# Half as many opening products on TensorE, each twice as wide

## The chip, the cores and the metric

The kernel runs on one core of a Trainium2 chip, in one launch. The time is the device time of that core in microseconds (us), the median of several runs. The profile is of one separate execution, and times inside it are counted from its first instruction.

## The reference

One transformer block on 2048 rows of width 512, in bfloat16: a pre-norm linear attention with 32 heads of 16, and a pre-norm dense block of width 1792 with a ReLU.

```python
def _A_ref(x, wqkv, wo):                       # linear attention
    qkv = (x @ wqkv).reshape(B, S, 3, H, Dh).transpose(2, 0, 3, 1, 4)
    q, k, v = qkv[0], qkv[1], qkv[2]
    phi = lambda t: jnp.where(t > 0, t + 1, jnp.exp(t)) + 1e-6
    pq, pk = phi(q), phi(k)
    kv = jnp.einsum("bhsd,bhse->bhde", pk, v)
    z = jnp.einsum("bhsd->bhd", pk)
    num = jnp.einsum("bhqd,bhde->bhqe", pq, kv)
    den = jnp.einsum("bhqd,bhd->bhq", pq, z)[..., None] + 1e-6
    return (num / den).transpose(0, 2, 1, 3).reshape(B, S, D) @ wo
...
h = x + _A_ref(_layernorm(x), A_wqkv, A_wo)
h2 = h + relu(_layernorm(h) @ B_w1) @ B_w2     # the result
```

## The kernel before

The 2048 rows are 16 tiles of 128, in four chunks of 512 rows. The program is a list of short words, `ORDER`, that is written out by hand. Each word is one step, a call of the function `op_` plus the word's name with the word's numbers, and the steps are recorded in the list's order; each engine runs its own instructions in that order, and waits on semaphores for what it needs. So the list fixes the order on every engine, SyncE's DMA issues among them, and nothing is rearranged later.

The steps at the start, which are those that the change and the prediction touch:

- `warm.n.b.w` (L243 to L245) runs n products on TensorE (PE) of a 128x128 block of zeros with w columns of zeros, into PSUM bank b. Nobody reads what they leave there; `start=True` makes the next user of the bank overwrite it. `warm.2.7` leaves w at 512. The zeros are the tile `zeros`, which is the first quarter of `m_sb`; `op_const` (L185) sets its first 128 columns with one VectorE memset (L186) and the other 384 with a later one (L190). Each product is a pair of instructions, a weight load (PEld) and a matmul.
- `lx` loads rows of x (L214), `lk` and `lq` the weights of k and q (`wk_sb`, `wq_sb`, L220), all by SyncE (SP), in the order of the list: x three times, wk, x three times, wq, and so on.
- `S`, `A`, `R`, `N` normalise a tile: statistics on VectorE (DVE; L248, L249), the inverse root on ScalarE (ACT; L254, L255), and the normalised tile into `h_nat` on VectorE (L262).
- `T` transposes a tile with four products of 128 columns (L287), `E` copies the transposed tile to `lnT` on ScalarE (L297).
- `K` is a tile's product with the k weights, four products of 512 columns (L316), `Q` a block of q for a whole chunk, four products of 512 (L324).

On TensorE the list begins: 70 products of 64 columns, two of 512, then T.0, T.1, K.0, T.2, K.1, T.3, K.2, and the first of the q products, Q.0.3, which is the first step that needs `wq_sb`. Behind it come more K and Q, the sum over all rows of k against the normalised tile (L368), small products for the attention's state (L392, L414, L426, L440), the attention's output (L493), and the dense block (L508 and L517 for its first product, L537 for its second). `wb` and `rb` (L468, L471) take the reciprocal of the denominators through DRAM into `rr`, and `dm` (L484) multiplies by it; each chunk's `h` products (L493) wait for that.

The only lines of the program that differ are the first warm word, and, in form alone, how `start` and `stop` of two products are computed.

Of the kernel before, what the change touches and what calls it, by code (L numbers as in the profile page):

```python
# [15 lines left out]


ORDER = """
table const masks warm.70.7.64 warm.2.7 lx.0.1 S.0 A.0 R.0.1 lx.1.1 S.1 lx.2.1 A.1 N.0 T.0.1 lk.0.4 S.2 R.1.1
N.1 T.1.2 lx.3.1 A.2 E.0 K.0.4 R.2.1 lx.4.2 S.3 N.2 T.2.1 E.1 A.3 S.5 R.3.1 K.1.0.0.2 K.1.0.2.2 N.3 S.4 A.5 A.4  # L20
E.2 T.3.2 K.2.6.0.2 K.2.6.2.2 F.0.1 M.0.1 lx.6.2 E.3 S.7 lq.0.4 R.4.2 lx.8.4 Q.0.3.1 N.4 U.0.1 A.7 F.1.1 F.2.1
T.4.2 N.5 S.6 Q.0.1.4 U.1.1 M.1.1 A.6 lx.12.4 M.2.1 D.0.1 R.6.2 K.3.7.0.2 K.3.7.2.2 E.4 X.5 U.2.1 U.3.1 D.1.1
N.6 Q.0.0.3 N.7 S.10 qF.0.0.2 K.4.5 K.5.6 S.8 A.10 S.9 A.8 qU.0.0.2 S.12 F.4.2 D.2.1 X.6 Q.0.2.0 A.9 A.12 K.6.2
S.13 S.11 M.4.2 A.11 A.13 U.4.2 D.4.2 F.3.1 R.8.2 N.9 M.3.1 X.7 K.7.3 R.12.2 R.10.2 N.8 F.6.2 D.3.1 N.13 S.15
G.0 G.1 U.6.2 S.14 X.9 X.8 N.10 A.14 A.15 N.12 qM.0.0.2 M.6.2 X.13 qF.0.2.2 R.14.2 qU.0.2.2 qM.0.2.2 N.11 G.2
G.3 G.5 G.4 N.14 X.12 K.9.3 K.8.2 K.13.1 N.15 qD.0.0.2 D.6.2 za.4.1 X.11 X.10 F.8.2 U.8.2 M.8.2 K.12.0 U.12.2
F.12.2 G.7 za.6.0 K.11.3 D.8.2 qD.0.2.2 M.12.2 za.8.0 K.10.2 F.10.2 X.14 G.8 K.14.0 U.10.2 X.15 K.15.1 M.10.2 zf
lv.2.2 lv.0.2 G.9 D.10.2 zhi D.12.2 F.14.2 G.6 G.10 G.11 M.14.2 zlo U.14.2 D.14.2 z.0.0 z.2.0 z.3.0 z.1.0 G.14
lo.0.2 lo.2.2 zc zh d4.0.1 dl4.0 l1.0.2 G.13 G.12 G.15 dx4.0 gA.2.2 Q.1.1.3 Q.1.0.2 qF.1.0.2 gD.0.2 kv.1.4
kv.3.4 kv.0.4 kv.2.4 kx qU.1.0.2 qM.1.0.2 qD.1.0.2 Q.1.3.1 Q.1.2.0 qF.1.2.2 m.0.2 m.1.3 mD.0.2 m.3.7 m.2.6 wb.0  # L30
Q.2.0.4 Q.2.1.5 rb.0.7 rb.0.1 rb.0.6 rb.0.3 rb.0.0 rb.0.2 rb.0.4 rb.0.5 l1.2.2 qM.1.2.2 qU.1.2.2 Q.2.3.1
qD.1.2.2 mA.2.2 qF.2.0.2 Q.2.2.0 qU.2.0.2 dm.0.2.2 dm.0.0.2 qM.2.0.2 h.1.6 hD.1 s.1 a.1 qU.2.2.2 d4.1.3 dl4.1
h.0.7 hD.0 s.0 dx4.1 h.2.6 h.3.5 a.0 l2.0.7 wb.1 hD.2 nA.1 hD.3 qF.2.2.2 nA.0 s.2 s.3 Q.3.0.2 Q.3.1.3 a.2
Q.3.3.6 a.3 qF.3.0.2 qU.3.0.2 Q.3.2.5 x.1 r.0.4 qF.3.2.2 n.2 t.2.7 n.3 t.3.4 qD.2.0.2 v.2 v.3 x.0 ph.0.3.1.0
ph.0.1.3.0 ph.0.2.0.0 ph.0.3.1.1 qM.2.2.2 qM.3.0.2 ph.0.0.2.0 ph.0.0.2.1 qM.3.2.2 qD.3.0.2 qU.3.2.2 qD.2.2.2
ph.0.2.0.1 qD.3.2.2 p.0.7.5 d4.2.6.2 pD.0.2.2 dl4.2 dl4.3 rb.1.4 rb.1.6 rb.1.3 rb.1.2 rb.1.0 rb.1.1 ph.0.1.3.1
rb.1.7 rb.1.5 p.0.6.4 dx4.2 dm.1.0.2 dm.1.2.2 h.4.0 pD.0.0.2 hD.4 pD.0.6.2 p.0.5.1 h.6.6 dx4.3 p.0.4.0 hD.6
l2.7.7 h.5.4 pA.0.4.2 s.4 s.6 hD.5 h.7.7 a.4 a.6 p.0.11.6 p.0.10.5 s.5 hD.7 a.5 p.0.9.4 wb.2 rb.2.6 n.4 rb.2.0
rb.2.4 s.7 n.6 rb.2.3 rb.2.2 rb.2.1 a.7 n.5 n.7 rb.2.5 rb.2.7 dm.2.0.2 dm.2.2.2 pD.0.10.2 p.0.13.1 p.0.12.0
p.0.8.3 pD.0.12.2 wb.3 r.4.4 rb.3.0 rb.3.4 h.10.7 hD.10 x.6 h.8.2 h.11.6 hD.8 s.10 rb.3.5 rb.3.1 rb.3.6  # L40
f.1.0.0.7 rb.3.3 rb.3.2 rb.3.7 s.8 hD.11 pD.0.8.2 h.9.5 f.3.1.0.7 x.7 x.5 s.11 a.8 hD.9 f.1.0.7.7 f.0.4.0.7 a.10
a.11 x.4 dm.3.2.2 dm.3.0.2 h.14.7 h.12.3 s.9 n.11 h.15.6 a.9 n.10 h.13.2 fo.1 n.9 n.8 hD.14 s.14 hD.12 x.11
hD.15 f.0.4.7.7 r.8.4 p.1.13.7 p.1.6.3 a.14 hD.13 s.12 s.15 s.13 a.12 a.15 a.13 n.14 p.1.12.6 n.13 f.3.1.7.7
n.12 n.15 p.1.2.5 fo.0 pD.1.12.2 x.10 p.1.7.4 fo.3 p.1.3.6 x.9 pD.1.6.2 pD.1.2.2 r.12.4 x.8 p.1.11.2 p.1.10.1
pD.1.10.2 f.2.4.0.7 p.2.0.6 p.2.1.7 f.2.4.7.7 pD.2.0.2 p.2.10.0 p.2.11.1 fo.2 x.14 p.2.6.2 p.2.7.3 x.15 fd.3
p.2.13.7 p.2.12.6 pD.2.10.2 pD.2.6.2 x.12 fd.1 pD.2.12.2 p.2.2.0 x.13 fd.0 p.2.3.1 p.1.5.6 p.1.4.5 pD.2.2.2
pD.1.4.2 p.1.0.3 p.1.1.4 p.1.9.1 p.1.8.0 pD.1.0.2 pD.1.8.2 f.4.4.0.7 f.4.4.7.7 fo.4 fd.4 f.5.3.0.7 f.5.3.7.7
fo.5 fd.2 f.6.7.0.7 f.6.7.7.7 fo.6 p.2.4.2 p.2.5.3 f.7.0.0.7 f.7.0.7.7 pD.2.4.2 fo.7 p.3.6.1 p.3.7.2 pD.3.6.2
p.3.8.3 p.3.9.4 p.3.5.1 pD.3.8.2 p.3.4.0 pD.3.4.2 fd.6 p.3.10.3 p.3.11.4 pD.3.10.2 p.3.2.0 p.3.3.1 p.3.0.5
p.3.1.6 pD.3.2.2 pD.3.0.2 p.3.13.3 fd.7 p.3.12.2 pD.3.12.2 f.10.1.0.7 f.15.2.0.14.3.1 f.15.7.0.14.0.2 p.2.8.4  # L50
p.2.9.5 fo.15.3.1 fd.15.3.1 fo.15.0.2 pD.2.8.2 f.8.7.0.7 f.10.1.7.7 fo.10 f.8.7.7.7 fo.8 f.14.2.0.7 f.14.2.7.7
f.13.3.0.7 fd.5 fd.8 fd.10 fo.14 f.13.3.7.7 fo.13 f.9.0.0.7 f.9.0.7.7 fd.15.0.2 f.11.6.0.7 f.11.6.7.7 fd.13 fo.9
f.12.0.0.7 fd.9 f.12.0.7.7 fo.11 fd.14 fd.11 fo.12 fd.12 f.15.2.0.14.2.1 fo.15.2.1 fd.15.2.1
"""


# [1 line left out]
def kernel(  # L58
# [14 lines left out]
    S, D = xf.shape  # L73
# [7 lines left out]
    KD = D // P  # L81
    KF = FF // P
# [5 lines left out]
    const = ctx.enter_context(tc.tile_pool(name="const", bufs=1))  # L88
# [58 lines left out]
    rb = big.tile([P, NE, 2, CW], BF16, name="rb")  # L147
# [10 lines left out]
    def pk(t, n=1):  # L158
        return pk_lo[:, t : t + n, :] if t < 2 else acts[0][:, t - 2 : t - 2 + n, :]
# [9 lines left out]
    z_on = lambda n: z_sb.rearrange("p (k o) -> p k o", o=1).broadcast_to([P, KD, n])  # L169
    at_bank = {}  # L170
    summed, stated = set(), set()
    dsts = {"k": lambda t, n: pk(t, n), "q": lambda i, n: pqT[i // KD][:, i % KD : i % KD + n, :]}
    unit = {"k": 0, "q": NT}

# [137 lines left out]
    def op_K(t, b, k=0, n=KD):  # L312
        c, j = divmod(t, CT)
        at_bank["k", t] = b
        for kd in range(k, k + n):
            nc.tensor.matmul(  # L316
                bk[:, b, :], lhsT=lnT[c][:, kd, j * P : (j + 1) * P], rhs=wk_sb[:, kd, :],
                start=(kd == 0), stop=(kd == KD - 1),
            )

    def op_Q(c, j, b):
# [211 lines left out]
    def op_f(t, b, f0, n, k=0, w=KD):  # L533
        c, j = divmod(t, CT)
        at_bank["f", t, k] = b
        for f in range(f0, f0 + n):
            nc.tensor.matmul(  # L537
                bk[:, b, 0 : w * P], lhsT=acts[c % 2][:, f, j * P : (j + 1) * P],
                rhs=w2_sb[:, f, k * P : (k + w) * P],
                start=(f == 0), stop=(f == KF - 1),  # L540
            )

    def op_fo(t, k=0, w=KD):
# [44 lines left out]
```

## Time and profile before

| | |
|---|---|
| time, median of 3 runs | 169.89 us (169.71 to 170.19) |
| span of the profiled execution, first to last instruction | 168.0 us |
| the profiled execution's own time | its page gives the span alone |
| median less span | 1.9 us |
| TensorE, matmuls busy | 162.7 us, 97% of the span, 924 products |
| TensorE, weight loads busy | 79.2 us, 47%, 924 loads |
| VectorE busy | 115.6 us, 69% |
| ScalarE busy | 49.5 us, 29% |
| instructions in all | 2417 |
| DMA | 16.01 MB, mean 95 GB/s |

A busy PE is a modelled figure: a product's recorded time goes from its issue to the modelled end of its passage through the array, and the next one begins to stream before that. What one costs in a row of many is the distance between starts. PEld is the weight load, which runs beside the products. In the list of waits, "A <- B" says that A sat idle until B was done.

### The profile page before, as it was taken

To read this page: it belongs to the slowest core of one execution; us is meant where nothing else is said; L and a number is where in the kernel's file an instruction comes from. 1 tells how busy PE (TensorE), PEld (TensorE's weight loads), DVE (VectorE), ACT (ScalarE), POOL (GpSimd) and SP (SyncE) were. 2 spreads that over 40 slices of the span, in tenths; PEclk is the share of its full clock that TensorE was granted. 3 is DMA by queue.
4 is the path that set the end of the run, shared out by engine and by line. 5 is a ranking of instruction groups with operands and counts; after the bars stand their busy time and mean duration, and the time that the engine had idled before them with its cause. 6 is when DMAs were issued, how large, how long until landed. Compare 5 with 4: busy or idle time off the path is not lost.

```text
span 168.0 us, 2417 instructions
## 1 busy us (share of the span) xinstructions
PE 162.7 (97%) x924; PEld 79.2 (47%) x924; DVE 115.6 (69%) x217; ACT 49.5 (29%) x83; POOL 4.8 (3%) x21
## 2 busy tenths in 40 slices
PE   7799999999999999999999999999999999999992
PEld 7444444454544754444444444444444447444442
DVE  3899999942579999999999755764144773432312
ACT  3799968715798843100101000000000000000000
POOL 7400000000000000000000000000000000000000
PEclk9999999999999999999999999999999999999999
DMA  4984054681595364414552520000101000011021
GB/s 108 353 298 88 20 106 95 189 301 45 132 337 161 98 205 132 132 48 123 83 102 57 126 63 0 0 0 0 62 31 35 0 0 7 32 34 48 31 94 39
DMA packets 25003, 16.01 MB, mean 95 GB/s; under 512 B 15008, under 2 KB 23968, under 8 KB 24992
## 3 DMA queue, kind: packets, MB, share of 16 engines
q1 hardware_dynamic: 24992, 15.87, 33.2%
q8 instruction: 7, 0.11, 0.3%
q14 instruction: 4, 0.03, 0.1%
HBM read 9.96 MB, written 2.62 MB: 75 GB/s over the span
## 4 chain that ended last, share of the span: by engine, by line
PE 92%; DMA 4%; SPq 2%; DVE 1%; issue 0%
PE bk L537 28%; PE bk L508 27%; PE bk L324 8%; PE bk L368 8%; PE bk L493 8%; PE bk L316 7%; DMA wq_sb<-in_A_wqkv_dram 4%; PE bk L517 2%; SPq L214 2%; PE bk L440 1%; DVE gT L545 1%; PE bk L392 1%; PE bk L414 1%; PE bk L426 1%; PE bk L287 0%
## 5 line engine op out<-in xcount | busy, mean ns | idle before, releaser
L537 PE MATMUL bk<-w_sb,at 128*128 128x512 bf16 (+2 forms) x252 | 50.0, 355 | 0.0
L508 PE MATMUL bk<-lnT,w_sb 128*128 128x512 bf16 x208 | 46.9, 379 | 0.0
L528 DVE TENSOR_SCALAR at<-bk 128x1024 bf16<-128x1024 f32 x27 | 32.8, 1223 | 13.2 <-PE bk L508 13.2
L537 PEld LDWEIGHTS <-at 128*128 128x128 bf16 x252 | 23.5, 98 | 25.4
L508 PEld LDWEIGHTS <-w_sb 128*128 128x128 bf16 x208 | 20.4, 98 | 23.9
L545 DVE SCALAR_TENSOR_TENSOR gT<-bk,rstd,h_nat 128x512 bf16<-128x512 f32 (+2 forms) x18 | 12.4, 691 | 24.6 <-PE bk L537 22.0
L334 ACT ACTIVATE eb<-bk 128x1024 bf16<-128x1024 f32 (+1 forms) x18 | 16.6, 929 | 5.3 <-PE bk L316 2.8
L337 ACT ACTIVATE rb<-bk 128x1024 bf16<-128x1024 f32 (+1 forms) x18 | 16.4, 929 | 0.0
L324 PE MATMUL bk<-lnT,wq_sb 128*128 128x512 bf16 x64 | 15.1, 379 | 0.3 <-DMA wq_sb<-in_A_wqkv_dram 0.3
L316 PE MATMUL bk<-wk_sb,lnT 128*128 128x512 bf16 x64 | 15.3, 379 | 0.0
L493 PE MATMUL bk<-m_sb,pqs 128*128 128x512 bf16 x64 | 15.1, 379 | 0.0
L368 PE MATMUL bk<-at,h_nat 128*128 128x512 bf16 x56 | 13.1, 379 | 0.0
L248 DVE BATCH_NORM_STATS2 st<-x_nat 128x6 f32<-128x512 bf16 x16 | 10.6, 678 | 2.3 <-DMA x_nat<-in_A_x_dram 2.3
L499 DVE TENSOR_TENSOR h_nat<-bk,x_nat 128x512 bf16<-128x512 f32 x16 | 10.6, 676 | 0.9 <-PE bk L493 0.9
L254 ACT ACTIVATE rstd<-mv,eps 128x2 f32<-128x2 f32 (+2 forms) x14 | 4.2, 297 | 23.7 <-DVE mv L251 20.9
L250 DVE BATCH_NORM_STATS2 st<-h_nat 128x6 f32<-128x512 bf16 x16 | 10.5, 684 | 0.1
L324 PEld LDWEIGHTS <-wq_sb 128*128 128x128 bf16 x64 | 6.1, 98 | 7.7 <-DMA wq_sb<-in_A_wqkv_dram 0.8
L493 PEld LDWEIGHTS <-pqs 128*128 128x128 bf16 x64 | 6.1, 98 | 7.7 <-DVE pqs L484 0.6
L368 PEld LDWEIGHTS <-h_nat 128*128 128x128 bf16 x64 | 6.1, 98 | 7.3 <-issue 0.2
L316 PEld LDWEIGHTS <-lnT 128*128 128x128 bf16 x64 | 6.1, 98 | 6.8
L341 DVE TENSOR_SCALAR eb<-eb 128x1024 bf16<-128x1024 bf16 (+1 forms) x18 | 6.6, 389 | 0.0
L262 DVE TENSOR_SCALAR h_nat<-x_nat,mv,rstd 128x512 bf16<-128x512 bf16 x16 | 6.3, 408 | 0.2 <-ACT rstd L255 0.2
(65 smaller groups left out, 87.7 us busy)
## 6 DMA issues: line engine op xcount, KB each, us to landing
w_sb<-in_B_w_dram SPq DMA_DIRECT2D x4, 896.0 KB, 6.2
rr<-scr SPq DMA_DIRECT2D x32, 64.0 KB, 2.6
out_dram<-gT SPq DMA_DIRECT2D x15, 128.0 KB, 1.9
x_nat<-in_A_x_dram SPq DMA_DIRECT2D x2, 512.0 KB, 7.9
x_nat<-in_A_x_dram SPq DMA_DIRECT2D x4, 128.0 KB, 2.2
wk_sb<-in_A_wqkv_dram SPq DMA_DIRECT2D x1, 512.0 KB, 4.1
x_nat<-in_A_x_dram SPq DMA_DIRECT2D x2, 256.0 KB, 4.6
wq_sb<-in_A_wqkv_dram SPq DMA_DIRECT2D x1, 512.0 KB, 6.2
```

The lines of the kernel that those rows point to most:

```text
L248: op_S = lambda t: nc.vector.bn_stats(out=st[:, t, :], in_=x_nat[:, t, :])
L316: nc.tensor.matmul(bk[:, b, :], lhsT=lnT[c][:, kd, j * P : (j + 1) * P], rhs=wk_sb[:, kd, :], start=(kd == 0), stop=(kd == KD - 1),)
L324: nc.tensor.matmul(bk[:, b, :], lhsT=wq_sb[:, kd, j * P : (j + 1) * P], rhs=lnT[c][:, kd, :], start=(kd == 0), stop=(kd == KD - 1),)
L334: nc.scalar.activation(out=buf(eb, kind, i, n), in_=bank(at_bank[kind, i], n), func=ACT.Exp)
L337: nc.scalar.activation(out=buf(rb, kind, i, n), in_=bank(at_bank[kind, i], n), func=ACT.Relu)
L368: nc.tensor.matmul(bk[:, KD + kd, :], lhsT=ln_nat[:, t, kd * P : (kd + 1) * P], rhs=pk(t)[:, 0, :], start=(not stated), stop=(len(stated) ...
L493: nc.tensor.matmul(bk[:, b, :], lhsT=pqs[:, (c * KD + jb) % NQ, j * P : (j + 1) * P], rhs=m_sb[:, jb, :], start=(jb == 0), stop=(jb == KD ...
L499: nc.vector.tensor_tensor(out=h_nat[:, t : t + n, :], in0=bank(at_bank["h", t], n), in1=x_nat[:, t : t + n, :], op=ALU.add,)
L508: nc.tensor.matmul(bk[:, b, :], lhsT=w1_sb[:, kd, f * P : (f + 1) * P], rhs=lnT[c][:, kd, :], start=(kd == 0), stop=(kd == KD - 1),)
L528: nc.vector.tensor_scalar(out=acts[c % 2][:, f : f + n, :], in0=bank(at_bank["p", c, f], n), scalar1=-1.0, scalar2=0.0, op0=ALU.mult, op1= ...
L537: nc.tensor.matmul(bk[:, b, 0 : w * P], lhsT=acts[c % 2][:, f, j * P : (j + 1) * P], rhs=w2_sb[:, f, k * P : (k + w) * P], start=(f == 0), ...
L545: nc.vector.scalar_tensor_tensor(out=o_t[:, t % NO, cols], in0=bk[:, at_bank["f", t, k], 0 : w * P], scalar=rstd2[:, t : t + 1], in1=h_nat ...
```

## The change

The first warm word `warm.70.7.64` becomes `warm.35.7.128`: 35 products of 128 columns in place of 70 of 64. The columns streamed are the same, 4480; so are the bank, the block of zeros, the two products of 512 columns behind them, and every other word. The new width reads columns 0 to 127 of `zeros`, which the first memset (L186) sets, so the products wait for the same memset as before. TensorE has 35 weight loads and 35 matmuls fewer, 70 instructions; the instructions of the other engines, and TensorE's own behind the warm words, stand in the same order with the same waits.

The diff also changes how `op_K` and `op_f` say which product is the first and which the last of a sum. With this list both forms give the same flags. Lines behind it are numbered 6 or more higher in the kernel after.

```diff
-table const masks warm.70.7.64 warm.2.7 lx.0.1 S.0 A.0 R.0.1 lx.1.1 S.1 lx.2.1 A.1 N.0 T.0.1 lk.0.4 S.2 R.1.1
+table const masks warm.35.7.128 warm.2.7 lx.0.1 S.0 A.0 R.0.1 lx.1.1 S.1 lx.2.1 A.1 N.0 T.0.1 lk.0.4 S.2 R.1.1 N.1
...
+    fed = {}
+
+    def part(key, n):
+        at = fed[key] = fed.get(key, 0) + 1
+        return {"start": at == 1, "stop": at == n}
+
...
             nc.tensor.matmul(
                 bk[:, b, :], lhsT=lnT[c][:, kd, j * P : (j + 1) * P], rhs=wk_sb[:, kd, :],
-                start=(kd == 0), stop=(kd == KD - 1),
+                **part(("k", t), KD),
             )
...
-                start=(f == 0), stop=(f == KF - 1),
+                **part(("f", t, k), KF),
```

More of the change, by code (lines that the diff above doesn't have):

```diff
@@ L18 @@
 ORDER = """
-table const masks warm.70.7.64 warm.2.7 lx.0.1 S.0 A.0 R.0.1 lx.1.1 S.1 lx.2.1 A.1 N.0 T.0.1 lk.0.4 S.2 R.1.1
[L20 to L53, printed above, removed]
+table const masks warm.35.7.128 warm.2.7 lx.0.1 S.0 A.0 R.0.1 lx.1.1 S.1 lx.2.1 A.1 N.0 T.0.1 lk.0.4 S.2 R.1.1 N.1
@@ new lines @@
+T.1.2 lx.3.1 A.2 E.0 K.0.4 R.2.1 lx.4.2 S.3 N.2 T.2.1 E.1 A.3 S.5 R.3.1 K.1.0.0.2 K.1.0.2.2 N.3 S.4 A.5 A.4 E.2
+T.3.2 K.2.6.0.2 K.2.6.2.2 F.0.1 M.0.1 lx.6.2 E.3 S.7 lq.0.4 R.4.2 lx.8.4 Q.0.3.1 N.4 U.0.1 A.7 F.1.1 F.2.1 T.4.2
+N.5 S.6 Q.0.1.4 U.1.1 M.1.1 A.6 lx.12.4 M.2.1 D.0.1 R.6.2 K.3.7.0.2 K.3.7.2.2 E.4 X.5 U.2.1 U.3.1 D.1.1 N.6
+Q.0.0.3 N.7 S.10 qF.0.0.2 K.4.5 K.5.6 S.8 A.10 S.9 A.8 qU.0.0.2 S.12 F.4.2 D.2.1 X.6 Q.0.2.0 A.9 A.12 K.6.2 S.13
+S.11 M.4.2 A.11 A.13 U.4.2 D.4.2 F.3.1 R.8.2 N.9 M.3.1 X.7 K.7.3 R.12.2 R.10.2 N.8 F.6.2 D.3.1 N.13 S.15 G.0 G.1
@@ new lines @@
+U.6.2 S.14 X.9 X.8 N.10 A.14 A.15 N.12 qM.0.0.2 M.6.2 X.13 qF.0.2.2 R.14.2 qU.0.2.2 qM.0.2.2 N.11 G.2 G.3 G.5 G.4
+N.14 X.12 K.9.3 K.8.2 K.13.1 N.15 qD.0.0.2 D.6.2 za.4.1 X.11 X.10 F.8.2 U.8.2 M.8.2 K.12.0 U.12.2 F.12.2 G.7
+za.6.0 K.11.3 D.8.2 qD.0.2.2 M.12.2 za.8.0 K.10.2 F.10.2 X.14 G.8 K.14.0 U.10.2 X.15 K.15.1 M.10.2 zf lv.2.2
+lv.0.2 G.9 D.10.2 zhi D.12.2 F.14.2 G.6 G.10 G.11 M.14.2 zlo U.14.2 D.14.2 z.0.0 z.2.0 z.3.0 z.1.0 G.14 lo.0.2
+lo.2.2 zc zh d4.0.1 dl4.0 l1.0.2 G.13 G.12 G.15 dx4.0 gA.2.2 Q.1.1.3 Q.1.0.2 qF.1.0.2 gD.0.2 kv.1.4 kv.3.4 kv.0.4
@@ new lines @@
+kv.2.4 kx qU.1.0.2 qM.1.0.2 qD.1.0.2 Q.1.3.1 Q.1.2.0 qF.1.2.2 m.0.2 m.1.3 mD.0.2 m.3.7 m.2.6 wb.0 Q.2.0.4 Q.2.1.5
+rb.0.7 rb.0.1 rb.0.6 rb.0.3 rb.0.0 rb.0.2 rb.0.4 rb.0.5 l1.2.2 qM.1.2.2 qU.1.2.2 Q.2.3.1 qD.1.2.2 mA.2.2 qF.2.0.2
+Q.2.2.0 qU.2.0.2 dm.0.2.2 dm.0.0.2 qM.2.0.2 h.1.6 hD.1 s.1 a.1 qU.2.2.2 d4.1.3 dl4.1 h.0.7 hD.0 s.0 dx4.1 h.2.6
+h.3.5 a.0 l2.0.7 wb.1 hD.2 nA.1 hD.3 qF.2.2.2 nA.0 s.2 s.3 Q.3.0.2 Q.3.1.3 a.2 Q.3.3.6 a.3 qF.3.0.2 qU.3.0.2
+Q.3.2.5 x.1 r.0.4 qF.3.2.2 n.2 t.2.7 n.3 t.3.4 qD.2.0.2 v.2 v.3 x.0 ph.0.3.1.0 ph.0.1.3.0 ph.0.2.0.0 ph.0.3.1.1
@@ new lines @@
+qM.2.2.2 qM.3.0.2 ph.0.0.2.0 ph.0.0.2.1 qM.3.2.2 qD.3.0.2 qU.3.2.2 qD.2.2.2 ph.0.2.0.1 qD.3.2.2 p.0.7.5 d4.2.6.2
+pD.0.2.2 dl4.2 dl4.3 rb.1.4 rb.1.6 rb.1.3 rb.1.2 rb.1.0 rb.1.1 ph.0.1.3.1 rb.1.7 rb.1.5 p.0.6.4 dx4.2 dm.1.0.2
+dm.1.2.2 h.4.0 pD.0.0.2 hD.4 pD.0.6.2 p.0.5.1 h.6.6 dx4.3 p.0.4.0 hD.6 l2.7.7 h.5.4 pA.0.4.2 s.4 s.6 hD.5 h.7.7
+a.4 a.6 p.0.11.6 p.0.10.5 s.5 hD.7 a.5 p.0.9.4 wb.2 rb.2.6 n.4 rb.2.0 rb.2.4 s.7 n.6 rb.2.3 rb.2.2 rb.2.1 a.7 n.5
+n.7 rb.2.5 rb.2.7 dm.2.0.2 dm.2.2.2 pD.0.10.2 p.0.13.1 p.0.12.0 p.0.8.3 pD.0.12.2 wb.3 r.4.4 rb.3.0 rb.3.4 h.10.7
@@ new lines @@
+hD.10 x.6 h.8.2 h.11.6 hD.8 s.10 rb.3.5 rb.3.1 rb.3.6 f.1.0.0.7 rb.3.3 rb.3.2 rb.3.7 s.8 hD.11 pD.0.8.2 h.9.5
+f.3.1.0.7 x.7 x.5 s.11 a.8 hD.9 f.1.0.7.7 f.0.4.0.7 a.10 a.11 x.4 dm.3.2.2 dm.3.0.2 h.14.7 h.12.3 s.9 n.11 h.15.6
+a.9 n.10 h.13.2 fo.1 n.9 n.8 hD.14 s.14 hD.12 x.11 hD.15 f.0.4.7.7 r.8.4 p.1.13.7 p.1.6.3 a.14 hD.13 s.12 s.15
+s.13 a.12 a.15 a.13 n.14 p.1.12.6 n.13 f.3.1.7.7 n.12 n.15 p.1.2.5 fo.0 pD.1.12.2 x.10 p.1.7.4 fo.3 p.1.3.6 x.9
+pD.1.6.2 pD.1.2.2 r.12.4 x.8 p.1.11.2 p.1.10.1 pD.1.10.2 f.2.4.0.7 p.2.0.6 p.2.1.7 f.2.4.7.7 pD.2.0.2 p.2.10.0
@@ new lines @@
+p.2.11.1 fo.2 x.14 p.2.6.2 p.2.7.3 x.15 fd.3 p.2.13.7 p.2.12.6 pD.2.10.2 pD.2.6.2 x.12 fd.1 pD.2.12.2 p.2.2.0 x.13
+fd.0 p.2.3.1 p.1.5.6 p.1.4.5 pD.2.2.2 pD.1.4.2 p.1.0.3 p.1.1.4 p.1.9.1 p.1.8.0 pD.1.0.2 pD.1.8.2 f.4.4.0.7
+f.4.4.7.7 fo.4 fd.4 f.5.3.0.7 f.5.3.7.7 fo.5 fd.2 f.6.7.0.7 f.6.7.7.7 fo.6 p.2.4.2 p.2.5.3 f.7.0.0.7 f.7.0.7.7
+pD.2.4.2 fo.7 p.3.6.1 p.3.7.2 pD.3.6.2 p.3.8.3 p.3.9.4 p.3.5.1 pD.3.8.2 p.3.4.0 pD.3.4.2 fd.6 p.3.10.3 p.3.11.4
+pD.3.10.2 p.3.2.0 p.3.3.1 p.3.0.5 p.3.1.6 pD.3.2.2 pD.3.0.2 p.3.13.3 fd.7 p.3.12.2 pD.3.12.2 f.10.1.0.7
@@ L54 @@
+f.15.2.0.14.3.1 f.15.7.0.14.0.2 p.2.8.4 p.2.9.5 fo.15.3.1 fd.15.3.1 fo.15.0.2 pD.2.8.2 f.8.7.0.7 f.10.1.7.7 fo.10
+f.8.7.7.7 fo.8 f.14.2.0.7 f.14.2.7.7 f.13.3.0.7 fd.5 fd.8 fd.10 fo.14 f.13.3.7.7 fo.13 f.9.0.0.7 f.9.0.7.7
+fd.15.0.2 f.11.6.0.7 f.11.6.7.7 fd.13 fo.9 f.12.0.0.7 fd.9 f.12.0.7.7 fo.11 fd.14 fd.11 fo.12 fd.12
+f.15.2.0.14.2.1 fo.15.2.1 fd.15.2.1
 """
```

## The prediction

> **What bounds the kernel now.** I read the page's totals first, then a table of stretches of TensorE (PE), the chain that ended last, and the list of who made PE wait.
>
> ```profile
> span 168.0 us, 2417 instructions
> PE 162.7 (97%) x924; PEld 79.2 (47%) x924; DVE 115.6 (69%) x217; ACT 49.5 (29%) x83; POOL 4.8 (3%) x21
> PEclk9999999999999999999999999999999999999999
> ```
>
> PE is busy for 97% of the span, so the question is where the other 3% lies. The stretches say (length, busy time, products that ran in it, clock, DMA):
>
> ```profile
> 1.04:4.24 3.20, 3.19 (x60) 1.00 0.60 144
> 4.24:4.54 0.30, 0.30 (x14) 1.00 0.85 239
> 4.54:5.04 0.50, 0.50 (x8) 1.00 0.99 336
> 5.04:10.36 5.32, 4.07 (x29) 1.00 1.07 380
> 10.36:164.96 154.60, 154.59 (x824) 1.00 0.31 85
> 164.96:167.95 2.99, 0.01 (x1) 1.00 0.18 55
> ```
>
> From 10.36 to 164.96 us PE has no gap, and 2.99 us of output lie behind it. The 824 products of the long stretch are the same in both kernels. So the end is fixed by two things alone: when that unbroken row begins, and whether it stays unbroken. What begins it is in the chain that ended last (start, length, what) and in PE's waits (total, times, longest):
>
> ```profile
> 4.16 6.17 DMA wq_sb<-in_A_wqkv_dram
> 10.38 1.04 PE bk L324 x4
> 11.41 0.22 PE bk L287 x4
> 11.63 0.86 PE bk L324 x4
> ...
> PE bk L245 <- DVE m_sb L186: 1.1, 1, 1.1
> PE bk L287 <- DVE h_nat L262: 0.9, 2, 0.6
> PE bk L324 <- DMA wq_sb<-in_A_wqkv_dram: 0.3, 1, 0.3
> ```
>
> The row begins with the first q product, and that waits for the q weights, issued by SP at 4.16 and landed at 10.33 (4.16 + 6.17). The opening products (L245) are not in the chain at all. They matter only if they, or the clock that they leave behind, hold up what PE must finish before 10.38.
>
> **The opening products now.** The groups of the first stretch by shape, and lines of the timeline up to the first q product:
>
> ```profile
> L245 PE MATMUL bk<-m_sb 128*128 128x64 bf16 x60 | 3.4, 242 | 1.1 <-DVE m_sb L186 1.1
> ...
> 4.54 0.59 PE L245 MATMUL bk<-m_sb 128*128 128x512 bf16 x2
> ...
> 4.65 0.38 DVE L262 TENSOR_SCALAR h_nat<-x_nat,mv,rstd 128x512 bf16<-128x512 bf16 x1
> 5.09 0.23 PEld L287 LDWEIGHTS <-h_nat 128*128 128x128 bf16 x4 [0.45 <-DVE h_nat L262]
> ...
> 9.02 1.03 PE L316 MATMUL bk<-wk_sb,lnT 128*128 128x512 bf16 x4
> ...
> L414 PE MATMUL bk<-gT,wv_sb 128*128 128x128 bf16 x16 | 1.1, 219 | 0.0
> ...
> 42.42 0.89 PE bk L414 x16
> ```
>
> Sixty of the 70 products of 64 columns begin in the first 3.20 us: one every 3.20 / 60 = 53.3 ns. The other ten begin between 4.24 and 4.54, where the first of the 512-column products starts: one every 30 ns. So PE runs at about half speed to 4.24 us and at full speed behind that, although the clock columns above say 9 and 1.00 from the start; I go by the distances. Four products of 512 take 0.86 us at full speed (third PE line of the chain), 0.216 each, so the two opening ones are through the array's input at 4.54 + 0.43 = 4.97. The first transpose then waits for VectorE's normalised tile (4.65 + 0.38 = 5.03) and starts at 5.09. PE thus has 0.12 us to spare at that point, and the end of the opening is not what releases the first transpose.
>
> [...]
>
> **The change, part by part.**
>
> *Width at half speed.* No row has a 128-column product at half speed. By columns it takes twice the 64-column one, 106.7 ns. Below that: at full speed the 16 products of L414, 128 columns each, take 0.89 us, 55.6 ns each, which is 1.85 times the 30 ns of 64 columns, so 99 ns. Above: if the weight load didn't fit beside a single product, its recorded mean in the opening could set the distance:
>
> ```profile
> L245 PEld LDWEIGHTS <-m_sb 128*128 128x128 bf16 x72 | 3.6, 126 | 1.0 <-DVE m_sb L186 1.0
> ```
>
> That is 126 ns. I take 106.7, since today's loads of 126 ns stand 53 ns apart and so already overlap each other.
>
> *The sum at the opening.* With 106.7 ns, 30 products start by 4.24 (3.20 / 0.1067), and the other five take 5 x 55.6 = 0.28 us: the 512-column ones start at 4.52 against 4.54 now, a shift of -0.02 us. With 99 ns: 32.3 by 4.24, 2.7 left, 4.39, or -0.15. With 126 ns: 25.4 by 4.24, 9.6 left at the 98 to 126 ns of a load, up to 1.2 us, 5.45 in place of 4.54, or +0.91.
>
> *What of it reaches the end.* The gains none: the first transpose waits for VectorE at 5.03. The loss of 0.91 would push the first transpose to 5.45 + 0.43 = 5.88, by 0.79 us. Work that PE has between there and 10.38, by the groups of the first 11 us:
>
> ```profile
> L316 PE MATMUL bk<-wk_sb,lnT 128*128 128x512 bf16 x12 | 3.1, 379 | 0.0
> L287 PE MATMUL bk<-ident,h_nat 128*128 128x128 bf16 x16 | 1.6, 222 | 0.9 <-DVE h_nat L262 0.9
> ```
>
> Twelve products of 512 at 0.216 and sixteen transposes at 0.056 stream for 2.59 + 0.89 = 3.48 us, in a stretch of 5.32: 1.84 us of room, which is what covers a late opening. Even 0.79 fits. So each of the three prices comes out at nothing by 10.38. If the cover were gone, each would cost its full shift.
>
> *Seventy instructions fewer on PE.* Nothing is queued that gets past a wait: both kernels stop at the same transposes, for the same tile. Cost nothing in the stream; what it moves is when code is fetched, a rival below. *SP, VectorE, ScalarE, GpSimd:* their instructions are the same, so the q weights are issued at 4.16 as now. *Bank 7* isn't read after the opening, and its next writer stands behind the q weights. *The `start`/`stop` form* leaves the same flags: nothing.
>
> Sum: 168.0 us of span + 0.0. The runs' median of 169.89 lies 1.9 us above the span, and holds what lies before the first and behind the last instruction; I carry that over: 169.9 us.
>
> **The rivals.**
>
> *Full clock comes too late (slower).* If wider and fewer products counted for less in whatever raises the clock, PE would stay at half speed behind 4.24. The opening would then last to 1.04 + 35 x 0.1067 + 0.85 = 5.63 (the two products of 512 at twice 0.216), and the 3.48 us of work behind it, at half speed, 6.96 more, to 12.59. If full speed comes at time g, the rest takes half: the work ends at g + (12.59 - g)/2 = 6.3 + g/2. That passes 10.38, and so moves the end, from g = 8.2 us on; at g = 10.4 the row begins at 11.5, +1.1 us, 171.0; every further us adds half. Against it: PE was busy for 3.19 of 3.20 us before the clock rose, and it will be as busy in the same 3.20 us with the same columns. I see nothing that would delay it by 4 us. For it: only one execution shows when the clock rises. [...] Chance 0.14.
>
> *Code fetches land badly (slower).* The queue of instruction fetches, over the whole execution and in one stretch of 2 us (11 to 13), with the waits on the transfers through DRAM:
>
> ```profile
> q8 instruction: 7, 0.11, 0.3%
> q8 instruction: 1, 0.02, 3.4%
> ...
> PEld L493 <- DVE pqs L484: 0.6, 2, 0.3
> DVE pqs L484 <- DMA rr<-scr: 0.2, 1, 0.2
> ...
> L471 SPq DMA_DIRECT2D rr<-scr x32: 303/424/529, 41.2 to 77.8; - x32
> ```
>
> Seven fetches of about 16 KB; one takes 3.4% of 16 engines for 2 us, 1.1 us of one of them. PE has 1848 of the 2417 instructions, so I take these for PE's, some 264 instructions each (estimate). Seventy instructions are 35 products, at 0.216 us 7.6 us: each fetch would come that much later, at other neighbours. One that sat in front of an `rr` transfer, between 41 and 78 us, could hold it up by 1.1 us, and the `h` products (L493) behind it, which today wait 0.6 us on PE's loads for `pqs` with PE itself still busy. One such collision, half of it covered: +0.55, 170.4; two: 171.0. Against it: none of the seven fetches leaves a gap in PE's 154.60 us today, and one of them falls into that stage already. Chance 0.11.
>
> *The row begins earlier (faster).* K.2's four products start at 9.02 and are in by 9.88; the q product follows at 10.38. If the q weights landed sooner, at most 0.50 us could go, and by the recorded wait 0.33: 169.4 at best. Nothing in the change touches the q weights' queue. A larger gain is possible only if the runs of before, unlike the profiled one, already pay for a late clock. Chance 0.11.
>
> *The change does nothing that is not in the diff's words* is the forecast itself: same columns, same time, same neighbours. Chance 0.64.
>
> **How the numbers follow.** What a measurement of this kernel can tell from no change is about 0.3%, 0.5 us; the three runs span 0.48. The forecast case alone holds 169.4 to 170.4. The slower cases start at 170.4 and lie mostly below 171; I take the range to 170.9, and down to 169.3 for the faster one, leaving out the farther part of the late clock and of the faster case, less than 0.2. Slower by over 0.3%: 0.14 + 0.11 = 0.25. Faster: 0.11. Same: 0.64.
>
> **What would show it.** In the profile after: 35 products of 128 columns some 107 ns apart, then about five some 56 ns apart; the first 512-column product between 4.4 and 4.6; the first transpose at 5.1, released by VectorE; PE's wait for the q weights still about 0.3 us; the long stretch 154.6 us with no gap. The prediction is wrong in its first step if the opening ends behind 5.1 with PE's transposes no longer waiting; in its clock step if the transposes and k products behind it stand 107 and 427 ns apart; in its fetch step if PE shows new gaps between 41 and 78 us; and in its bound if the time moves by over 0.5 us while the q weights land and the row begins as before.

## The result, and the profile after

The changed kernel takes 171.3 us (median of 4 runs, 170.96 to 171.75) against 169.84: a ratio of 1.0096, 95% interval 1.0073 to 1.0119. It is slower by about 1%, 1.5 us, where no change was forecast, and the time lies above the range. The profiled execution was the longest of the four, 171.75 us, so the losses read from it come out a little larger than those of the median.

Its page, its stretches (cut where the row of products begins and ends) and TensorE's waits:

```profile
span 170.0 us, 2331 instructions
PE 163.1 (96%) x873; PEld 79.7 (47%) x889; DVE 115.8 (68%) x217; ACT 49.4 (29%) x83; POOL 4.7 (3%) x21
...
10.72:167.02 156.30, 154.29 (x809) 1.00 0.31 83
167.02:170.02 3.00, 0.00 (x1) 1.00 0.18 55
...
PE bk L251 <- DVE m_sb L192: 1.1, 1, 1.1
PE bk L322 <- DMA lnT<-h_nat: 0.6, 1, 0.6
PE bk L499 <- DVE pqs L490: 0.6, 1, 0.6
PE bk L322 <- ACT lnT L303: 0.4, 1, 0.4
PE bk L293 <- DVE h_nat L268: 0.2, 1, 0.2
PE bk L330 <- ACT rstd L261: 0.2, 1, 0.2
```

The long row had no gap before; now TensorE is idle in it, with two waits of 0.6 us: one of K's products (L322) for a transposed tile, and one of the attention's output (L499) for `pqs`. (A few of its products have no record in this trace, so busy times are slightly low; the waits are not made by that.) The two places in the timeline:

```profile
16.36 0.81 PE L330 MATMUL bk<-lnT,wq_sb 128*128 128x512 bf16 x3
17.76 0.82 PE L322 MATMUL bk<-wk_sb,lnT 128*128 128x512 bf16 x3 [0.59 <-DMA lnT<-h_nat]
...
63.33 0.81 PE L514 MATMUL bk<-lnT,w_sb 128*128 128x512 bf16 x3
64.73 0.61 PE L499 MATMUL bk<-m_sb,pqs 128*128 128x512 bf16 x2 [0.59 <-DVE pqs L490]
```

By distances between starts, less the 0.216 us that a product takes, the losses are 0.76 at 17, 0.76 and 0.16 at 64. The row began at 10.73 in place of 10.38, 0.35. Together 2.03, of the 2.07 us by which the two profiled spans differ (170.02 less 167.95).

What stands beside both waits is a code fetch, a packet of the queue that the page calls `q8 instruction`; by their records seven fetches of 16,384 bytes, one packet each, began at 11.4, 35.5, 51.4, 71.0, 97.6, 126.2 and 149.4 us before, and at 14.7, 38.3, 59.6, 82.5, 107.2, 136.5 and 158.5 after. A second queue that the page calls one of instructions, q14, has packets of 8,192 bytes; in this profile they began at 19.9, 45.0, 71.6 and 83.6 us, beside neither wait.

### The profile page after: what moved, and what is told of

Read it like the earlier page. It is cut to its first block, busy times and chain, and to the rows that moved or that the text cites. A ratio compares the mean times of both kernels' runs of the same rounds, so it can differ in the third digit from the quotient of the medians.

```text
span 170.0 us, 2331 instructions
## 1 busy us (share of the span) xinstructions
PE 163.1 (96%) x873; PEld 79.7 (47%) x889; DVE 115.8 (68%) x217; ACT 49.4 (29%) x83; POOL 4.7 (3%) x21
## 4 chain that ended last, share of the span: by engine, by line
PE 79%; DMA 7%; DVE 5%; SPq 3%; ACT 3%; issue 1%; DVEq 0%
PE bk L543 28%; PE bk L514 25%; PE bk L374 8%; PE bk L499 7%; PE bk L322 5%; PE bk L330 4%; DMA x_nat<-in_A_x_dram 3%; DMA lnT<-h_nat 2%; SPq L477 2%; DMA rr<-scr 2%; DVE st L256 2%; DVE h_nat L505 1%; ACT eb L340 1%; SPq L220 1%; DVE gT L551 1%
## 5 line engine op out<-in xcount | busy, mean ns | idle before, releaser
L514 PE MATMUL bk<-lnT,w_sb 128*128 128x512 bf16 x202 | 46.4, 379 | 0.3
L322 PE MATMUL bk<-wk_sb,lnT 128*128 128x512 bf16 x61 | 15.0, 379 | 1.1 <-DMA lnT<-h_nat 0.6
L499 PE MATMUL bk<-m_sb,pqs 128*128 128x512 bf16 x63 | 15.3, 380 | 0.6 <-DVE pqs L490 0.6
L499 PEld LDWEIGHTS <-pqs 128*128 128x128 bf16 x64 | 6.0, 98 | 8.7 <-DVE pqs L490 1.8
L322 PEld LDWEIGHTS <-lnT 128*128 128x128 bf16 x64 | 6.0, 98 | 8.3 <-DMA lnT<-h_nat 1.3
```

The source lines that it names most:

```text
L322: nc.tensor.matmul(bk[:, b, :], lhsT=lnT[c][:, kd, j * P : (j + 1) * P], rhs=wk_sb[:, kd, :], **part(("k", t), KD),)
L499: nc.tensor.matmul(bk[:, b, :], lhsT=pqs[:, (c * KD + jb) % NQ, j * P : (j + 1) * P], rhs=m_sb[:, jb, :], start=(jb == 0), stop=(jb == KD ...
L514: nc.tensor.matmul(bk[:, b, :], lhsT=w1_sb[:, kd, f * P : (f + 1) * P], rhs=lnT[c][:, kd, :], start=(kd == 0), stop=(kd == KD - 1),)
```

## The experiments

**The theories.** F: the 70 instructions that are gone move TensorE's code fetches, and two of the seven now meet transfers that TensorE soon needs. W: the wide products, or the moment at which the clock rises behind them, hold the kernel up. D: the first loads just had bad luck in one execution. The kernels differ from the changed one, or from the kernel before where that is said, only in what is shown. The table collects the profiled executions: the first, third and fourth fetch, the start of the q row, and the gaps behind it (distance between starts, less the product's own time), all in us. Where a text says when the clock rose, that is the trace's record of the full granted clock (from 4.26 us on in the first profile before, from 6.29 in the first after); starts of products about half as far apart agree with it. Ratios are to the kernel before, with their 95% intervals.

| run | opening | fetches 1, 3, 4 | row | gaps | ratio, 95% |
|---|---|---|---|---|---|
| before | 70x64 | 11.4, 51.4, 71.0 | 10.38 | none | |
| after | 35x128 | 14.7, 59.6, 82.5 | 10.73 | 17: 0.76; 64: 0.92 | 1.0096, 1.0073 to 1.0119 |
| e1 | 35x120, 35x8 | 11.5, 51.7, 71.3 | 10.59 | none | 1.0009, 0.9993 to 1.0024 |
| e2 | 35x128 | 14.4, 58.5, 82.3 | 10.15 | 17: 0.97; 64: 0.75 | 1.0098, 1.0071 to 1.0125 |
| e3 | 70x32 | 11.0, 51.7, 71.3 | 10.61 | 73: 0.87 | 1.0074, 1.0053 to 1.0094 |
| e4 | 35x64 | 15.2, 59.7, 82.3 | 10.87 | 17: 0.69; 64: 0.92 | 1.0128, 1.0105 to 1.0151 |
| g1 | 35x128, later 35x1 | 11.6, 51.9, 71.0 | 10.56 | none | 1.0020, 1.0003 to 1.0036 |
| f90 | 90x50 | 7.0, 47.5, 70.5 | 10.65 | 31: 1.31; 51: 1.28 | 1.0176, 1.0136 to 1.0217 |
| f53 | 53x85 | 11.9, 52.2, 76.8 | 10.04 | 57: 0.38; 83: 0.79 | 1.0058, 1.0028 to 1.0089 |
| d1 | 70x64, extra copy | 11.5, 51.4, 70.8 | 10.11 | 63: 0.16 | 1.0030, 1.0007 to 1.0052 |
| h1 | 35x128, 35x1 at 45 us | 14.7, 52.7, 72.7 | 10.85 | 17: 0.31 | 1.0110, 1.0076 to 1.0144 |
| b1 | 70x64 | 11.2, 51.6, 70.6 | 10.36 | none | one profile |
| b2 | 70x64 | 11.7, 51.2, 70.8 | 9.97 | 73: 0.93 | one profile |
| f66 | 66x68 | 11.6, 52.0, 74.8 | 10.14 | none | 1.0013, 0.9993 to 1.0033 |

**e1: the instruction count back, the columns kept.**

```diff
-table const masks warm.35.7.128 warm.2.7 lx.0.1
+table const masks warm.35.7.120 warm.35.7.8 warm.2.7 lx.0.1
```

> 35 products of 120 columns and 35 of 8 in the opening: the 4480 columns of both kernels, but the 70 pairs of instructions of the kernel before. Theory F (code fetch: 70 instructions fewer move each of TensorE's seven code fetches by 3 to 11 us, onto the transfers that feed the transposed tiles at 17 us and the rr transfers at 60 us): fetches back at about 11, 35, 51, 71 us, no gap of 0.7 us at 17 and at 64 us, 169.9 us within 0.4. Theory W (wide products raise the clock later, and that holds the kernel up): wide products as in the changed kernel, so clock up at about 6.3 us and 171.3 us. Theory D (only the luck of the first loads in one execution): no rule, anything from 169.8 to 171.7 with a spread like the changed kernel's.

169.56 against 169.43 us: the loss is gone, and with it both gaps, and the fetches are where they were. As F said.

**e2: the changed kernel once more.**

> The changed kernel once more, for a second profile on the same chip as the others. F: 171.3 us, fetches at about 14.7, 38, 60, 82 us, a gap near 17 us and one near 64 us whenever the clock rises. W: 171.3 us, clock again up behind 6 us. D: the gaps stand at other places or are gone, and the time differs by up to 1 us from 171.3.

171.1 us, with both gaps. In this execution the clock rose at 4.21 us, as early as in the profile of the kernel before, and the row of q products began at 10.15, earlier than before. The opening went as the prediction had it (groups by shape of 1.04 to 4.18, and the timeline):

```profile
L251 PE MATMUL bk<-m_sb 128*128 128x128 bf16 x30 | 3.3, 312 | 1.0 <-DVE m_sb L192 1.0
...
4.50 0.59 PE L251 MATMUL bk<-m_sb 128*128 128x512 bf16 x2
...
10.14:166.48 156.34, 154.30 (x810) 1.00 0.32 85
166.48:169.47 2.99, 0.00 (x1) 1.00 0.18 55
```

Thirty products in the first 3.2 us, the 512-column ones at 4.50: a good start. Yet the row takes 156.34 us in place of 154.60: 1.74 us lost in it, and 0.24 won back by the early start. Neither the width nor the clock can be what costs. How the transfers fare shows in SP's issues from 11 to 20 us and from 55 to 64 us (count, ns least/median/most of one issue, then us from issue to landing). The kernel before:

```profile
L308 SPq DMA_TRANSPOSE lnT<-h_nat x4: 1189/1204/1831, 11.1 to 19.4; - x4
DMA to landing us min/median/max: 2.4/2.4/3.4
...
L471 SPq DMA_DIRECT2D rr<-scr x8: 418/424/448, 55.6 to 58.9; - x8
DMA to landing us min/median/max: 2.8/3.0/3.0
```

The changed kernel, in e2:

```profile
L314 SPq DMA_TRANSPOSE lnT<-h_nat x4: 1188/1238/2113, 11.3 to 19.3; - x4
DMA to landing us min/median/max: 2.4/3.0/4.0
...
L477 SPq DMA_DIRECT2D rr<-scr x8: 418/425/1457, 56.3 to 60.7; - x8
DMA to landing us min/median/max: 2.7/2.9/3.7
...
q8 instruction: 1, 0.02, 3.9%
...
q8 instruction: 1, 0.02, 4.2%
```

The last two lines of this list are the queues of 14 to 16 and of 58 to 60 us: one fetch each, 3.9% and 4.2% of 16 engines' 2 us, 1.25 and 1.34 us of one engine. One issue of eight takes 1457 ns where the others take 425; it began at 58.70, 0.2 us behind the fetch at 58.5. One transpose's issue takes 2113; it began at 14.60, the fetch at 14.4. The chain that ended last in e2 tells which of these TensorE paid for:

```profile
13.31 4.03 DMA lnT<-h_nat
17.34 0.05 issue
17.39 1.47 PE bk L322 x6
...
58.69 1.46 SPq L477
60.15 0.04 issue
60.20 0.43 SPq L477
60.62 0.04 issue
60.66 2.66 DMA rr<-scr
```

At 64 us it is the long issue: SP issues in order, the two `rr` issues behind it start a microsecond late (60.20 and 60.66), and the last of them lands in its usual time, 2.66 us. At 17 us it is not. TensorE waited for the transpose before the long one, issued at 13.31 in its usual 1188 ns, which landed after 4.03 us in place of 2.4; the fetch began 1.1 us behind that issue. The first profile after is the same (issued at 13.65, landed after 4.06). Before, the first fetch met a transpose too (issue of 1831 ns, from 11.10, landed after 3.4, the fetch at 11.4), but that tile was needed late enough, and no fetch lay between 55 and 64.

The trace also has the 16 updates of its semaphore by which each `rr` transfer reports its landing. Over the 14 profiles here, 407 `rr` transfers had no q8 fetch running between issue and landing: the sixteenth update came at most 0.57 us behind the fifteenth, and none landed after more than 3.2 us. Fourteen transfers landed later than that behind an issue of ordinary length, all of them with a fetch in between. In 13 of them the sixteenth update came 0.6 to 2.0 us behind the other fifteen; in one, of f66, fifteen were late. These 13 belong to eight fetches, and each time the first of them was complete 1.04 to 1.27 us behind the end of the fetch's packet. So a fetch here held up one sixteenth of a transfer until it was itself through. A late transpose's updates all come late together (from 17.45 to 17.71 us for the one that TensorE waited for in the first profile after), and tell nothing of this.

**e3 and e4: half the columns, with either count.**

```diff
-warm.35.7.128
+warm.70.7.32      (e3)
+warm.35.7.64      (e4)
```

> 70 products of 32 columns: the instruction count of the kernel before with half the columns, so the opening is shorter and TensorE idles before the first transpose. F: 169.9 us within 0.4, fetches as before the change, even if the clock rises later, so long as it does by 8 us. W: less work in the opening, clock up later than 4.3 us, slower than before by 0.5 us or more. D: no rule.

> 35 products of 64 columns: the instruction count of the changed kernel with half its columns. F: fetches as in the changed kernel (14.7, 38, 60 us) and 171.3 us within 0.4. W: even less work before the first transpose, clock up later than in the changed kernel, 171.5 us or more. D: no rule.

e4 has the changed kernel's fetches and gaps, and a clock that rose only at 9.27 us. It takes 171.77 us, just outside F's band and inside W's, 0.3% more than the changed kernel by the ratios. That part fits W, if not its 1%: the q weights had landed at 10.13, and TensorE itself came to the q products only at 10.87. e3, with the clock up at 8.55, is a miss for F as I put it and within W's band: 0.74% slower. There too TensorE came late, at 10.61 with the weights landed at 10.28; the larger part is a gap. Its profile has neither the gap at 17 nor that at 64 but one at 73 us, 0.87, beside a fetch at 71.3: the third chunk's last `rr` transfer took 4.16 us to land, from 69.17 on. The same fetch at 71.3 in e1, whose `rr` transfers were issued 0.23 us earlier (from 65.35, not 65.58), cost nothing. From the last `rr` issue to the fetch it is 2.13 us in e3 and 2.34 in e1. So small a shift goes with the difference, but b1 and b2 below show that it is not the moment alone.

**g1: the opening untouched, the count undone behind it.**

```diff
-E.0 K.0.4 R.2.1
+E.0 K.0.4 warm.18.7.1 R.2.1
...
-K.2.6.0.2 K.2.6.2.2 F.0.1
+K.2.6.0.2 K.2.6.2.2 warm.17.7.1 F.0.1
```

> The opening exactly as in the changed kernel (35 products of 128 columns, two of 512), and 35 products of one column put where TensorE idles before the first q product: 18 behind K.0, 17 behind K.2. Only the number of instructions ahead of 10.4 us is undone. Theory F (a code fetch that meets other transfers): fetches at about 11.5, 35.5, 51.5 and 71 us, no gap at 17 nor at 64 us, time within 0.3% of the kernel before. Theory W (the wide opening itself costs): as slow as the changed kernel, 1% over the kernel before.

```profile
PE bk L251 <- DVE m_sb L192: 1.1, 1, 1.1
PE bk L293 <- DVE h_nat L268: 0.8, 2, 0.6
...
L477 SPq DMA_DIRECT2D rr<-scr x8: 418/424/450, 55.7 to 59.1; - x8
...
10.13 0.57 PE L251 MATMUL bk<-m_sb 128*128 128x1 bf16 x17
10.56 0.81 PE L330 MATMUL bk<-lnT,wq_sb 128*128 128x512 bf16 x3
```

These are all of TensorE's waits, the issues from 55 to 64, and the timeline before the q row. With the very opening of the changed kernel the gaps are gone, and 0.8% of the 1% with them. What is left is 0.2% by the ratio, 0.6 us between the medians. The filler is a likely part of it: the q weights had landed at 9.94, and TensorE reached the q products 0.43 us late because of the 17 products themselves (10.13 to 10.56). This is the run that convicts the count alone: W, which has the wide opening cost 1%, is out.

**f90 and f53: other counts.**

```diff
-warm.35.7.128
+warm.90.7.50      (f90)
+warm.53.7.85      (f53)
```

> 90 products of 50 columns, 4500 columns: the fetches move the other way, to about 8, 31, 48 and 67 us. F: no gap at 17 nor at 64 us, but the fourth fetch now falls among the rr transfers of the third chunk (issued from 65 to 69 us), so an issue there takes over 1 us in place of 0.42, and a gap of up to 0.8 us follows at 70 to 75 us: 0.3 to 0.9 us slower than before; the first one may also delay the loads of x and wq, up to 0.5 more. If only the width mattered, more and narrower products would be no slower than the kernel before.

> 53 products of 85 columns, 4505 columns: fetches about half way, at 12 to 13, 36, 55 and 75 us. F: the second chunk's rr transfers (issued from 56 to 60 us) are met by their edge only and the gap at 64 us is smaller than in the changed kernel or gone; the fourth may meet the last chunk's rr transfers (73 to 78 us); time between the two kernels, 169.6 to 171. If the loss grew with the width alone, it would be about half of the changed kernel's, +0.5%, with the gaps at 17 and 64 us still there.

f90 is the slowest of all, 1.8%, with more and narrower products than either kernel: 3.3 us, where at most 1.4 was expected, and not by the gap that I had named. TensorE's waits in it:

```profile
PE bk L322 <- DMA lnT<-h_nat: 1.1, 1, 1.1
PE bk L499 <- DVE pqs L490: 1.1, 1, 1.1
...
PE bk L330 <- DMA wq_sb<-in_A_wqkv_dram: 0.5, 1, 0.5
```

Its second fetch, at 30.2, met a transpose (issued at 28.84 in 1223 ns, landed after 4.04 us), and the gap runs from 31 to 33; the load of `wv_sb` issued next, at 30.12, took 1682 ns. Its third, at 47.5, met the end of the first chunk's `rr` transfers, one of which took 4.6 us to land, and the gap is at 51. Its fourth came at 70.5, not at 67; it stretched an `rr` issue to 1393 ns as expected, but no gap followed. Both gaps have a fetch beside them, then, and not every meeting leaves a gap; my reckoning of where a fetch would fall did not hold. In f53 the fetch at 76.8 met the last chunk's `rr` issues (one of 2002 ns) and the gap is at 83; the one of 0.38 at 57, a wait that the profile puts down to ScalarE, isn't explained by a fetch. Its time, 170.76 us, is within what was expected.

**d1: the kernel before, with a copy of 16 KB put in.**

```diff
-x.1 r.0.4 qF.3.2.2
+x.1 r.0.4 blk.0 qF.3.2.2
...
+def op_blk(r):   # one_row: a scratch tile [1, 8192] in DRAM
+    nc.scalar.dma_start(out=one_row[:, :], in_=B_w2[r : r + 16, :].rearrange("(o a) n -> o (a n)", o=1))
```

> The kernel before with nothing changed in its opening, and one copy of 16 KB in DRAM issued by ScalarE at about 57.4 us, which adds nothing to the result. F: if the copy sits on one DMA engine as a code fetch does, it meets the rr transfers that are issued from 55.6 to 59.3 us, the last of them land up to 1.1 us later, and TensorE shows a gap of up to 0.8 us at 63 to 64 us: 0.3 to 0.9 us slower. If the copy is cut into many small packets over all engines, it costs under 0.1 us and tells nothing. Theory W: no change in either case.

```profile
q10 hardware_dynamic: 32, 0.02, 0.0%
...
L478 SPq DMA_DIRECT2D rr<-scr x8: 370/426/585, 55.3 to 58.8; - x8
DMA to landing us min/median/max: 2.6/2.8/3.0
```

The copy went out in 32 packets of 512 bytes; one issue took 585 ns, no landing was late, and the gap is 0.16 us. The time is up 0.3% (0.07 to 0.52%), more than the 0.1 us expected of this case, and the profile doesn't explain it. It is no imitation of a fetch, which is one packet of 16 KB. The same bytes in small packets left the landings alone, at 3.0 us at most. What it is in a fetch that holds a transfer up isn't shown: no run varied the size of its packet.

**h1: the count undone between the second and the third fetch.**

```diff
-Q.1.3.1 Q.1.2.0
+Q.1.3.1 warm.35.5.1 Q.1.2.0
```

> The changed kernel with 35 products of one column put into TensorE's row at about 45 us, behind the first two code fetches and ahead of the third. They cost TensorE 35 x 24.5 ns = 0.86 us (the distance of the one-column products of L392). Theory F, fetch by fetch: the first fetch stays at 14.5 us and its gap at 17 us stays (0.7 to 1.0 us); the third goes back from 58.5 to about 52 us and the gap at 64 us, with the rr issue of 1.5 us, is gone: about the changed kernel's time, 171.0, since 0.86 is paid for 0.75. If the two gaps had another common cause (late loads, clock), both stay and the time is 171.9.

```profile
PE bk L322 <- DMA lnT<-h_nat: 0.2, 1, 0.2
...
L477 SPq DMA_DIRECT2D rr<-scr x8: 418/424/445, 57.2 to 60.5; - x8
```

The third fetch went back to 52.7; the issues from 57 to 61 all take their 424 ns again, and the gap at 64 is gone. The first stayed at 14.7 and still stretched a transpose (1760 ns at 15.08); its gap is there but smaller than foretold, 0.31 against 0.76 in the first profile after. The tile that TensorE waited for landed earlier here (issued at 13.80, landed at 17.39, not 17.71; the fetch took 1.06 us and not 1.42), and TensorE came to it 0.12 us later. Last product: 1.67 us later than before, against 0.47 + 0.31 + 0.86 for the filler = 1.64. 171.34 us lies between the 171.0 of F and the 171.9 of one common cause; the trace decides, since one gap went with its fetch and the other stayed with its own. So the two gaps have one cause each.

**b1 and b2: the kernel before, two more profiles.**

> The kernel before again, for when the clock rises. Theory F: fetches at 11.5, 35.5, 51.5, 71 us and no gap behind 10.6 us wherever the clock rises up to 8 us. If a clock that rises after 6 us costs the changed kernel 0.5 us, it costs this one as much, and the span is 168.5.

> The same kernel once more, for another moment of the clock's rise: as for the run before it.

In b1 the clock rose at 6.70 us, 2.4 us later than in the first profile, and the span is 167.9, no longer than there. But the late clock used up all the room that there was: the q weights landed early here, at 10.11, and TensorE came to the q products at 10.36. In b2 it rose at 5.40, the row began early, at 9.97, and the span is 168.7:

```profile
PE bk L493 <- DVE pqs L484: 0.6, 1, 0.6
...
L471 SPq DMA_DIRECT2D rr<-scr x8: 310/417/433, 65.2 to 68.7; - x8
DMA to landing us min/median/max: 2.4/2.6/4.1
```

An `rr` transfer landed after 4.1 us in place of 2.6, next to the fetch at 70.8, and TensorE stood still at 73 as in e3. In b1 the fetch at 70.6 had the same neighbours, issued from 65.0 on, and none landed after more than 2.7 us; in both the last of them was issued 2.07 us before the fetch. What decides between the two stays open. The kernel before thus stands at the edge of the same trouble with its fourth fetch. F, as I wrote it, had no gap here.

**f66: off that edge?**

```diff
-warm.35.7.128
+warm.66.7.68
```

> 66 products of 68 columns, 4488 columns: eight instructions fewer than before, so each fetch comes up to about 0.9 us later: about 12, 36, 52.3 and 72 us. Theory F: the fourth fetch moves off the end of the third chunk's rr transfers (issued to 69 us, landed by 72), which it met in one of three profiles of the kernel before, and still ends before the next issues at 73.2; the first three stay clear. Median 0.0 to 0.2% under the kernel before, with fewer runs of 170.1 us or more. If it reaches the issues at 73 us, a gap of 0.3 to 0.8 us and 169.8 to 170.3. If the width alone mattered, no difference.

No difference: 169.62 against 169.47 us, ratio 0.9993 to 1.0033. The profile has no gap, and its fourth fetch at 74.8, further than forecast. That fetch did reach the issues at 73 us (one of 1141 ns, and a landing after 3.7 us), and still no gap followed. No version tried beats the kernel before.

## Why the prediction was wrong

- What bounds the kernel, and that only the row's start and its gaps can move the end: right. Row start and gaps account for 2.03 of the 2.07 us between the two profiled spans.
- The price of a 128-column product at half speed, 106.7 ns, and the opening's end at 4.52: right. Thirty started in the first 3.2 us and the 512-column ones followed at 4.50 where the clock rose at 4.21.
- "Seventy instructions fewer on PE ... Cost nothing in the stream; what it moves is when code is fetched": right as words. **The step that failed is the next one: the sum put the moved fetches at 0.0 us and left them to a rival.** They measured 0.76 at 17 us and 0.92 at 64 us in the first profile after, 0.97 and 0.75 in e2. The rival "code fetches land badly" has the mechanism and one of the two places (`rr`, issued from 55 to 60 us), and I gave it a chance of 0.11 and 0.55 us. It is the case that came, with the sign named for it, a new gap between 41 and 78 us. Two of its terms were mis-sized. The collision at `rr` was put at half of 1.1 us, and measured 0.75 to 0.92. And the first fetch was not weighed at all against the tile transposes that SP issues from 11 us on, because I looked only between 41 and 78 us; there it cost 0.69 to 0.97. Two collisions are what the rival priced at 171.0, and the time is 171.3; the range stopped at 170.9, below both.
- The shift of 7.6 us that the rival gave every fetch was wrong as well: the first two came 3.3 and 2.7 us later, the fourth 11.5.
- The argument against it, that no fetch leaves a gap today, proved little. That all seven fall well goes with this count of instructions, and the trace already showed them at work: the first stretched a transpose's issue to 1831 ns, and beside the fourth a write to `scr` took 3.96 us to land, where the same write took 2.3 in b1. In b2 one of them falls badly even in the kernel before.
- Full clock too late: not what cost the 1%, as e2 has both gaps with the clock up at 4.21. But its price of zero up to 8.2 us was too kind. The formula counts only PE's own work behind the opening, and leaves out its waits for VectorE and ScalarE. In b1, with the clock up at 6.70, TensorE came to the q products at 10.36, where the formula has 9.65. That cost nothing against the first profile of before, whose row begins at 10.38; the row of b2 began at 9.97. The sum at the opening took the rise at 4.24 us for the changed kernel too. No run shows a fixed moment: it varied from execution to execution, 3.73 to 6.70 us over the profiles of openings with some 4480 columns, and in the first profile after it came at 6.29, in e2 at 4.21.
- The moment at which the row begins moved between 9.97 and 10.85 in the profiles other than e4, in kernels of either kind. Where it was late it was mostly the q weights: in the first profile after they landed at 10.68, and the row began at 10.73. So the 0.35 of that profile goes with the landing of the weights, which the change does not touch; e2 began earlier than before and lost as much in its row.

TensorE itself didn't wait for a fetch, as far as its waits show: for each wait in its row the profile names another releaser. It was the transfers of others that paid, and through them TensorE, 1% of the time. The fetches' records last 0.88 to 1.47 us in the first profiles of before and after. How a fetch comes to hold up one sixteenth of a transfer no run here shows, and why an issue by SP is stretched stays open too.

## What to carry to other kernels

In this kernel, with no slack in TensorE's row, adding or removing TensorE instructions early in the program moved the later code fetches (the first from 11.4 us to 14.7 with 70 fewer, to 7.0 with 40 more), and some of them got in the way of other transfers, for 0.69 to 0.97 us at each of the two places in the changed kernel and e4. Look in the trace where the instruction queue's packets fall, and which issue or landing beside them is long; then follow the chain to see which of these was waited for, since the longest need not be the one. When an edit that should be neutral costs 1%, first restore the instruction count with harmless fillers; if the loss goes, the edit itself is innocent. And a rival that is physically there but "leaves no gap today" deserves its price at every place that it can reach, not only at the one that was looked at.

## What the runs showed of the hardware that was not expected

- Beside a fetch, single issues by SP took 1.14 to 2.00 us in place of 0.42 (`rr`) and as much as 2.24 in place of 1.2 (transposes). Landings took as much as 4.6 us in place of 2.6 (`rr`) and 4.06 in place of 2.4 (transposes).
- Of an `rr` transfer that a fetch met, one sixteenth was late and the rest on time, in 13 of 14 late landings with an ordinary issue.
- The fetches don't move in proportion to the instructions. Four pairs fewer (f66) moved the fourth from 71.0 to 74.8 us, the third only from 51.4 to 52.0; 35 pairs fewer moved the first by 3.0 to 3.8 us and the fourth by 11. The fetch is thus not tied to the instruction that runs at that moment; to what, stays open.
- With half of the columns in the opening the clock rose at 8.55 and 9.27 us, against 3.73 to 6.70 with all of them.
